# A recurrent attention followed by a top-1 mixture of experts: bonus coefficients from column-half matmuls of the transposed operands, and fp32 routing tables of two columns

## The chip, the cores and the metric

The kernel runs on one core of a Trainium2 chip. The metric is the device time of one execution in microseconds (us), from the first to the last instruction and what lies around them. Engines: PE (TensorE, matmuls; its weight loads are listed as PEld), DVE (VectorE), ACT (ScalarE), POOL (GpSimd) and SP (SyncE, which here only issues DMAs). Each engine works through its own list in order and waits on semaphores for the others.

## The reference

Two parts. An attention with a decaying state, over 4 batches, 8 heads, 768 positions and a head size of 48:

```python
for t in range(S):
    kt, vt, rt = (k[:, :, t], v[:, :, t], r[:, :, t])
    cur = np.einsum('bhd,bhe->bhde', u[None] * kt, vt)
    y[:, :, t] = np.einsum('bhd,bhde->bhe', rt, state + cur)
    state = w[None, :, :, None] * state + np.einsum('bhd,bhe->bhde', kt, vt)
```

The term with `u` is the bonus: position t's own v, times the number sum over d of r·u·k. This number is the bonus coefficient, one for each position and head. The result x (3072 rows of 384) goes through a top-1 mixture of 8 experts (384 to 1024 to 384, ReLU between): each row goes to the expert with the largest logit x @ w_gate, and its output is scaled by the softmax weight of that expert and by a sigmoid of x @ w_output_gate.

## The kernel before, in words

The rows are cut into 24 tiles of 128 positions (4 batches of 6). The main loop takes one step for each tile, about 6.5 us. While the attention of tile i is worked out, the operands of later tiles are prepared and the logits of tile i-1 are taken. The order of all work on each engine is written out by hand: the list STEP names the parts of a step, and the parts are emitted in that order, so that each engine gets its instructions in it.

What the parts do, with the lines of the profile:

- "sc" (L277): scores of tile i, K·R, from the transposed operands RT and KT, in 64-column halves, into the PSUM tiles ps_a (two buffers).
- "a0", "a1" (L281): DVE masks the two score tiles into A.
- "in" (L315): the part of the output from the state T, into ps_y. It waits until DVE has read ps_y of the tile before (L330).
- "xt" (L372, L374): three PE transposes of the output x of tile i-1 into a PSUM tile that shares the two buffers of ps_a, then the ACT copy xT.
- "tr" (L264, L265): PE transposes of the scaled K and R of tile i+1, and the ACT copies KT and RT.
- "lm" (L382, L386): logits of tile i-1 from xT (PE), and their ACT copy lg. At the end of a group of four to six tiles the routing program of the group is started.
- "i0", "i1" (L323): A·v into ps_y. "st" (L293 on PE, L301 or L298 on DVE, L302 on POOL): the new state. Its PSUM tile ps_u and the logits' tile ps_l share the one buffer with the tag "u".
- "p0", "p1" (L217): DVE scales R and K of tile i+2 by tables of powers of w.
- "ut" (L239, L240): POOL forms k·u·r for tile i+2, 128 positions by 384. "bo" (L249 on DVE, L251 on POOL): DVE reduces it to the coefficients of tile i+1, 128 by 8, and POOL multiplies v by them, which gives vc.
- at the end of the step DVE adds ps_y and vc to x (L330), and SP stores x (L335). "ld" issues the loads of tile i+3.
- "m": DVE's place for the routing program. Each "m" gives a credit of 0.25 or 0.3, and each piece of the routing costs 0.15 to 0.6 of it. "t1": the place for the routing's matmuls on PE.

The routing of a group ranks its rows in their experts and writes, for each place in an expert's list, the row's number and its weight into a table, by a matmul of two 0/1 matrices (L534, ps_tab). In bf16 a number needs several columns to stay exact: the row number takes two (tile and row) and the weight three (parts, L459 to L464), so the right side has 5 × 32 columns.

From tile 18 on, each step ends with two pieces of work on the first expert's weights: ACT rounds half a block (L758), POOL forms the rest (L759). In step 22 the routing of the fourth group ends, and POOL gathers the first 256 rows of the first expert (L781); step 23 transposes them (L793). After the loop come the last group's routing, with the first expert's matmuls among it, and then the experts one after another (from about 190 us to the end), which the change does not touch.

Of the kernel before, what the change touches and what calls it, by code (L numbers as in the profile page):

```python
# [41 lines left out]
HB = 64  # L42
ORDER_AT = 14
# [4 lines left out]
STEP = ['m', 'sc', 'a0', 'm', 'a1', 'in', 'xt', 't1', 'm', 'tr', 't1', 'ld', 'ut', 'bo', 'm', 'p0', 'm', 'p1', 'lm', 'i0', 'st', 'i1', 'm']  # L48
# [4 lines left out]
STEP0 = ['sc', 'a0', 'm', 'a1', 'in', 'tr', 'ld', 'bo', 'm', 'p0', 'm', 'p1', 'i0', 'st', 'i1', 'm']  # L53
# [94 lines left out]
def make_powers(tc, pool, k, halfway):  # L148
# [22 lines left out]
    k.pr, k.pk, k.w128 = pr, pk, sq[7]  # L171

# [10 lines left out]
def load_rkv(tc, pin, spare, srcs, b, c, first, after=None):  # L183
    nc = tc.nc
    ts = []
    for nm, s in zip("krv", (srcs[1], srcs[0], srcs[2])):
        if nm in first:
            t = first[nm][:, :, :D]
        elif spare:
            t = spare.pop(0).rearrange("p (h d) -> p h d", h=H)  # L190
        else:
            t = pin.tile([C, H, D], F32, name=f"{nm}_t")
        nc.sync.dma_start(t, s[b, :, c * C : (c + 1) * C, :].rearrange("h p d -> p h d"))
        ts.append(t)
        if after and nm == "k":
            after()
    return [ts[1], ts[0], ts[2]]


class Attention:  # L200
    def __init__(self, tc, ctx, k, load, x_d):
        self.tc, self.k = tc, k
        self.load, self.x_d = load, x_d
        self.pw = ctx.enter_context(tc.tile_pool(name="att_w", bufs=2))
        self.T = None
        self.st, self.ku, self.vc, self.A = {}, {}, {}, [None, None]
# [26 lines left out]
    def uterm(self, i):  # L233
        if i >= NT:
            return
        nc, k = self.tc.nc, self.k
        rt, kt, vt = self.load(i)
        ku = self.pw.tile([C, H, D], F32, name="ku")
        nc.gpsimd.tensor_mul(ku, kt, k.u_b.rearrange("p (h d) -> p h d", h=H))  # L239
        nc.gpsimd.tensor_mul(ku, ku, rt)  # L240
        self.ku[i] = ku

    def bonus(self, i):
# [3 lines left out]
        vt = self.load(i)[2]  # L247
        coef = self.pw.tile([C, H], F32, name="coef")
        nc.vector.tensor_reduce(out=coef, in_=self.ku.pop(i), axis=AX.X, op=ALU.add)  # L249
        vc = self.pw.tile([C, H, D], F32, name="vc")  # L250
        nc.gpsimd.tensor_mul(vc, vt, coef.unsqueeze(2).to_broadcast((C, H, D)))  # L251
# [87 lines left out]
class Router:  # L339
# [54 lines left out]
    def group(self, ps, w, lg, i0, G, closing, last):  # L394
# [41 lines left out]
        def weighting():  # L436
# [20 lines left out]
            rest = scale  # L457
            for i in range(3):
                nc.vector.tensor_copy(parts[:, i], rest)  # L459
                yield  # L460
                if i < 2:
                    nxt = mk(f"rest{i}")
                    nc.vector.tensor_sub(nxt, rest, parts[:, i])
# [9 lines left out]
        nc.tensor.matmul(cnt, k.tri, oh16.rearrange("p c e -> p (c e)"), start=True, stop=(G == 1 and (first or based)), skip_group_check=True)  # L473
        if not first and not based:
            nc.tensor.matmul(cnt, k.ones16, rep(self.csum16), start=False, stop=(G == 1), skip_group_check=True)
        for c in range(G - 1):
            nc.tensor.matmul(cnt[:, (c + 1) * E :], k.ones16, oh16[:, c, :].unsqueeze(1).to_broadcast((C, G - 1 - c, E)), start=False, stop=(c == G - 2), skip_group_check=True)
# [33 lines left out]
        sel = hold("sel", W, dt=BF16)  # L511
# [7 lines left out]
        ohp = hold("ohp", QP, dt=BF16)  # L519
# [3 lines left out]
        rhs = hold("rhs", 5, W, dt=BF16)  # L523
        (nc.vector if last else nc.gpsimd).tensor_mul(rhs[:, :, 0], sel, bc(k.tile0[:, cols], W))
        nc.scalar.activation(rhs[:, :, 1], sel, AF.Copy, scale=k.row1)
        tab = self.tab

        def columns(i):
            nc.vector.tensor_mul(rhs[:, :, 2 + i], sel, bc(parts[:, i], W))

        def product(lo, hi):
            pt = ps.tile([C, 512], F32, name="ps_tab", tag="g", bufs=1)
            for c in range(G):
                nc.tensor.matmul(pt[:, lo * W : hi * W], ohp[:, c, :], rhs[:, c, lo:hi].rearrange("p a w -> p (a w)"), start=(c == 0), stop=(c == G - 1), skip_group_check=True)  # L534
            return pt

        def collect(pt, i):
# [7 lines left out]
        if last:  # L545
            yield P
            pt = product(0, 2)
            for i in range(2):
                yield V
                collect(pt, i)  # L550
# [26 lines left out]
            pt = product(2, 5)
            for i in range(2, 5):
                yield V
                collect(pt, i)  # L580
# [21 lines left out]
        collect(pt, 4)
# [9 lines left out]
    def early(self, pb):  # L612
        nc, k = self.tc.nc, self.k
        nc.tensor.matmul(pb[:, :E], k.ones16, self.csum16, start=True, stop=True, skip_group_check=True)
        nc.vector.scalar_tensor_tensor(self.base, self.pm0, float(EARLY * QP), pb[:, :E], op0=ALU.mult, op1=ALU.max)

    def order(self, ps, w):
# [3 lines left out]
        nc.tensor.matmul(pt[:, :E], k.ones, self.csum, start=True, stop=True)  # L621
# [524 lines left out]
def rwkv_top1_moe(ctx, tc, r, kk, v, w, u, wg, wog, w1, w2, out):  # L1146
# [5 lines left out]
    load_w(tc, const, w, k)  # L1152
# [3 lines left out]
    with ExitStack() as actx:  # L1156
# [14 lines left out]
        u_b = const.tile([C, DM], F32, name="u_b")  # L1171
        k.u_b = u_b
        load(1, lambda: nc.sync.dma_start(u_b, u.rearrange("h d -> (h d)").unsqueeze(0).to_broadcast((C, DM))))
        rw = actx.enter_context(tc.tile_pool(name="rw", bufs=1))
        with tc.manual_schedule(engines=ORDERED):
# [5 lines left out]
                for nm, sh, dt in (("lg", (2 * E,), F32), ("oh", (E,), F32), ("ex", (E,), F32), ("oh16", (E,), BF16), ("sel", (NQ * E,), BF16), ("ohp", (QP,), BF16), ("rhs", (5, NQ * E), BF16))  # L1181
# [62 lines left out]
        with tc.If(fast == 1) as cmp:  # L1244
            with ExitStack() as fctx:
# [33 lines left out]
                att.uterm(0)  # L1279
                att.uterm(1)  # L1280
                x, X = None, {}

                for i in range(NT):
# [8 lines left out]
                    def act(a):  # L1292
# [14 lines left out]
                        elif a == "ut":  # L1307
                            att.uterm(i + 2)
# [95 lines left out]
```

## Time and profile before

| | us |
|---|---|
| median of 3 runs | 425.01 |
| lowest, highest | 418.87, 426.81 |
| the profiled execution | 422.51 |
| its span, first to last instruction | 420.8 |
| busy in the span: PE, DVE, ACT, POOL | 372.9, 256.6, 152.1, 165.5 |

A row of the profile's groups reads: line, engine, operation, tile written <- tiles read, shapes, count | busy time, mean of one in ns | idle time of the engine before them, and what ended it. A row of the timeline reads: start, duration, engine, line, operation, tiles, count [idle before <- what ended it]. Several instructions of one kind that follow each other are merged into one row. A matmul in fp32 shows as two records, so that eight matmuls are 16.

### The profile page before, as it was taken

What the parts mean: (1) busy time and instruction counts of PE and PEld (TensorE: products, weight loads), DVE (VectorE), ACT (ScalarE), POOL (GpSimd) and SP (SyncE); (2) the same over time, 40 slices, a digit from 0 to 9 for tenths busy, and PEclk for the clock granted to TensorE, in tenths of its full rate; (3) what the DMA queues carried; (4) which work ended last, traced back from release to release, by engine and by line L of the source; (5) the groups of instructions that cost most, each with busy time, mean ns of one, the idle gap of its engine ahead of it and who ended that gap; (6) DMA issues with size and microseconds to landing.
All of it is one profiled execution on the core that took longest, in us unless ns stands there. A gap on an engine that the chain in (4) does not pass through costs nothing. (4 is left out here: it accounts for less than half of the span.)

```text
span 420.8 us, 11171 instructions
## 1 busy us (share of the span) xinstructions
PE 372.9 (89%) x4500; PEld 352.2 (84%) x4500; DVE 256.6 (61%) x592; ACT 152.1 (36%) x310; POOL 165.5 (39%) x215
## 2 busy tenths in 40 slices
PE   7799789878967696995998999999999999999990
PEld 4688678777867695995997999999999999999980
DVE  5878898989988963552875266266363663636300
ACT  2223232223232332421455265264453553625210
POOL 6967456555556644524041032222313503301010
PEclk8899899989979866896999999999999999999996
DMA  8957566646686611045528165174273552830010
GB/s 135 174 130 162 106 149 142 141 104 134 142 213 176 153 58 58 20 134 168 151 66 280 38 210 169 43 239 157 65 241 129 185 191 88 261 122 34 2 43 18
DMA packets 104696, 55.01 MB, mean 131 GB/s; under 512 B 78511, under 2 KB 102243, under 8 KB 104624
## 3 DMA queue, kind: packets, MB, share of 16 engines
q1 hardware_dynamic: 101200, 44.27, 41.2%
q0 software_dynamic: 3424, 9.82, 6.9%
q8 instruction: 40, 0.66, 0.6%
q14 instruction: 32, 0.26, 0.2%
HBM read 44.64 MB, written 9.76 MB: 129 GB/s over the span
## 5 line engine op out<-in xcount | busy, mean ns | idle before, releaser
L847 POOL DMA_INDIRECT out_dram<-yo,si x28 | 28.7, 1026 | 134.1 <-ACT yo L844 72.7
L810 PE MATMUL ps_h<-xh,w1h 128*128 128x384 f32 (+4 forms) x216 | 74.7, 346 | 6.0 <-issue 4.7
L811 PE MATMUL ps_h<-xl,w1h 128*128 128x384 f32 (+4 forms) x216 | 72.5, 336 | 0.0
L812 PE MATMUL ps_h<-xh,w1l 128*128 128x384 f32 (+4 forms) x216 | 72.4, 335 | 0.0
L781 POOL DMA_INDIRECT xg<-x_d,gi x28 | 31.2, 1115 | 46.0 <-PE ps_xt L793 31.1
L810 PEld LDWEIGHTS ps_h<-xh,w1h 128*128 128x128 f32 x216 | 42.6, 197 | 7.4 <-issue 5.0
L820 DVE SCALAR_TENSOR_TENSOR hl<-ps_h,hh 128x384 fp32r<-128x384 f32 (+4 forms) x72 | 38.0, 533 | 17.2 <-ACT hh L819 16.8
L819 ACT ACTIVATE hh<-ps_h 128x384 fp32r<-128x384 f32 (+4 forms) x72 | 33.7, 472 | 32.7 <-PE ps_h L812 32.7
L374 ACT COPY xT<-ps_x 128x384 f32<-128x384 f32 x24 | 11.5, 479 | 91.7 <-PE ps_x L372 83.6
L872 PE MATMUL ps_o<-w2h,hh 128*128 128x384 f32 x128 | 43.5, 340 | 0.0
L873 PE MATMUL ps_o<-w2l,hh 128*128 128x384 f32 x128 | 42.9, 335 | 0.0
L811 PEld LDWEIGHTS ps_h<-xl,w1h 128*128 128x128 f32 x216 | 42.7, 198 | 0.1
L874 PE MATMUL ps_o<-w2h,hl 128*128 128x384 f32 x128 | 42.8, 334 | 0.0
L812 PEld LDWEIGHTS ps_h<-xh,w1l 128*128 128x128 f32 x216 | 42.6, 197 | 0.2
L759 DVE TENSOR_TENSOR w1l<-raw,w1h 128x768 fp32r<-128x768 f32 x28 | 26.7, 955 | 23.4 <-ACT w1h L758 21.0
L758 ACT CAST w1h<-raw 128x768 fp32r<-128x768 f32 (+1 forms) x36 | 27.1, 764 | 27.0 <-PE ps_h L811 19.9
L281 DVE TENSOR_TENSOR A<-ps_a,mask 128x512 f32<-128x512 f32 x48 | 31.3, 683 | 5.7 <-PE ps_a L277 5.7
L796 DVE TENSOR_TENSOR xl<-ps_xt,xh 128x384 fp32r<-128x384 f32 (+4 forms) x27 | 13.9, 538 | 32.4 <-ACT xh L795 32.1
L251 POOL TENSOR_TENSOR vc<-v_t,coef 128x384 f32<-128x384 f32 x21 | 21.3, 1014 | 28.0 <-DVE coef L249 18.1
L759 DVE TENSOR_TENSOR w2l<-raw,w2h 128x768 fp32r<-128x768 f32 x28 | 26.7, 958 | 7.4 <-ACT w2h L758 5.7
L758 ACT CAST w2h<-raw 128x768 fp32r<-128x768 f32 (+1 forms) x36 | 26.7, 765 | 8.4 <-PE ps_o L874 4.4
L323 PE MATMUL ps_y<-v_t,A 128*64 128x48 f32 x672 | 29.3, 237 | 0.0
(224 smaller groups left out, 784.4 us busy)
## 6 DMA issues: line engine op xcount, KB each, us to landing
raw<-in_moe_w_dram SPq DMA_DIRECT2D x64, 384.0 KB, 3.5
x_d<-x SPq DMA_DIRECT2D x24, 192.0 KB, 1.9
v_t<-in_v_dram SPq DMA_DIRECT2D x21, 192.0 KB, 4.7
k_t<-in_k_dram SPq DMA_DIRECT2D x20, 192.0 KB, 3.0
r_t<-in_r_dram SPq DMA_DIRECT2D x20, 192.0 KB
raw<-in_v_dram SPq DMA_DIRECT2D x3, 192.0 KB
raw<-in_k_dram SPq DMA_DIRECT2D x3, 192.0 KB
xg<-x_d,gi POOLq DMA_INDIRECT x28, 4.7
```

Of the source, the lines that this page charges most:

```text
L281: self.tc.nc.vector.tensor_mul(a, self.pa[j], self.k.mask.unsqueeze(1).to_broadcast((C, NP, C)))
L758: nc.scalar.copy(hi, self.raw[i][:, cs])
L759: (eng or nc.vector).tensor_sub(lo, self.raw[i][:, cs], hi)
L781: nc.gpsimd.indirect_dma_start(out=self.xg[q][:n], out_offset=None, in_=self.x_d[:n_x, :], in_offset=bass.IndirectOffsetOnAxis(ap=self.rt. ...
L810: nc.tensor.matmul(o, wh[:, j, fs], xh, start=(j == 0), stop=False)
L811: nc.tensor.matmul(o, wh[:, j, fs], xl, start=False, stop=False)
L812: nc.tensor.matmul(o, wl[:, j, fs], xh, start=False, stop=(j == KC - 1))
L819: nc.scalar.activation(hh, o, AF.Relu)
L820: nc.vector.scalar_tensor_tensor(hl, o, 0.0, hh, op0=ALU.max, op1=ALU.subtract)
L872: nc.tensor.matmul(o, hh, wh, start=(f == 0), stop=False)
L873: nc.tensor.matmul(o, hh, wl, start=False, stop=False)
L874: nc.tensor.matmul(o, hl, wh, start=False, stop=(f == FC - 1))
```

## The change

The bonus coefficients come from PE. A new part "pr" lets POOL form P = RT·KT of tile i+1, 128 by 512, in the transposed layout; RT and KT carry powers of w that leave a factor 1/w in their product, so the new constant uw holds u·w, one column for each of the two heads in a 128-row block. "bo" is now eight matmuls of 64 columns of P by two columns of uw, into a PSUM tile with the tag "u", then an ACT copy of the coefficients, and eight ACT instructions that scale v, one for each head. "ut", the DVE reduce and the POOL multiply are gone. The load of u as a 128-row broadcast becomes two small loads into ut, issued ahead of the loads of tile 1.

The step has another order: "tr" comes ahead of "xt", "lm" and both "t1" stand around "i0" and "st", "bo" comes last, and there are five "m" in place of six.

The routing tables are fp32 with two columns (row number, weight): the parts, two of the columns and their collecting adds are gone. The routing matmuls run as pairs of 64-column halves.

```diff
-STEP = ['m', 'sc', 'a0', 'm', 'a1', 'in', 'xt', 't1', 'm', 'tr', 't1', 'ld', 'ut', 'bo', 'm', 'p0', 'm', 'p1', 'lm', 'i0', 'st', 'i1', 'm']
+STEP = ['m', 'sc', 'a0', 'm', 'a1', 'in', 'tr', 'xt', 'pr', 'ld', 'm', 'p0', 'm', 'p1', 'lm', 't1', 'i0', 'st', 't1', 'i1', 'm', 'bo']
-STEP0 = ['sc', 'a0', 'm', 'a1', 'in', 'tr', 'ld', 'bo', 'm', 'p0', 'm', 'p1', 'i0', 'st', 'i1', 'm']
+STEP0 = ['sc', 'a0', 'a1', 'tr', 'in', 'pr', 'ld', 'p0', 'p1', 'i0', 'st', 'i1', 'bo']
...
+    k.uw = pool.tile([C, NP, 2], F32, name="uw")
+    nc.gpsimd.memset(k.uw, 0.0)
+    for j in range(2):
+        rows = slice(HB * j, HB * (j + 1))
+        nc.gpsimd.tensor_mul(k.uw[rows, :, j], k.ut[rows], sq[0][rows])
...
-    def uterm(self, i):
...
-        nc.gpsimd.tensor_mul(ku, kt, k.u_b.rearrange("p (h d) -> p h d", h=H))
-        nc.gpsimd.tensor_mul(ku, ku, rt)
+    def product(self, i):
...
+        self.P = self.pw.tile([C, NP, C], F32, name="P", bufs=1)
+        self.tc.nc.gpsimd.tensor_mul(self.P, RT, KT)
...
+        pb = ps.tile([C, 512], F32, name="ps_b", tag="u", bufs=1)
+        for q in range(NP):
+            for c in range(2):
+                half = slice(HB * c, HB * (c + 1))
+                nc.tensor.matmul(pb[half, 2 * q : 2 * q + 2], self.P[:, q, half], self.k.uw[:, q, :], start=True, stop=True)
         coef = self.pw.tile([C, H], F32, name="coef")
-        nc.vector.tensor_reduce(out=coef, in_=self.ku.pop(i), axis=AX.X, op=ALU.add)
+        nc.scalar.copy(coef, pb[:, :H])
+        vt = self.st[i][2]
         vc = self.pw.tile([C, H, D], F32, name="vc")
-        nc.gpsimd.tensor_mul(vc, vt, coef.unsqueeze(2).to_broadcast((C, H, D)))
+        for h in range(H):
+            nc.scalar.activation(vc[:, h, :], vt[:, h, :], AF.Copy, scale=coef[:, h : h + 1])
...
-            rest = scale
-            for i in range(3):
-                nc.vector.tensor_copy(parts[:, i], rest)
...
+        for hf in halves:
+            nc.tensor.matmul(cnt[hf], k.tri[:, hf], oh16.rearrange("p c e -> p (c e)"), start=True, stop=(G == 1 and (first or based)), skip_group_check=True)
...
-        rhs = hold("rhs", 5, W, dt=BF16)
+        rhs = hold("rhs", 2, W)
...
+                for hf in HALVES:
+                    nc.tensor.matmul(pt[hf, lo * W : hi * W], ohp[:, c, hf], rhs[:, c, lo:hi].rearrange("p a w -> p (a w)"), start=(c == 0), stop=(c == G - 1), skip_group_check=True)
...
-                            if i == 0:
-                                att.bonus(0)
-                                att.uterm(2)
-                            att.bonus(i + 1)
+                            att.bonus(ps, i + 1)
```

How this moves the instructions is shown at three places, before and then after. The first is PE in an early step without routing, from the state part of the output ("in", ps_y<-T,RT) to the next step's scores; ps_t are the transposes of "tr", ps_x those of "xt", ps_l the logits, ps_u the state. The line numbers are those of the two kernels. Before:

```order
L315 MATMUL ps_y<-T,RT 64x48 x16
L372 MATMUL ps_x<-ident,x 128x128 x3
L264 MATMUL ps_t<-ident,Kn_300 128x128 x4
L264 MATMUL ps_t<-ident,Rn_297 128x128 x4
L382 MATMUL ps_l<-wg_151,xT 64x16 x6
L323 MATMUL ps_y<-v_t,A_675 64x48 x8
L293 MATMUL ps_u<-v_t,Kn_299 64x48 x8
L323 MATMUL ps_y<-v_t,A_677 64x48 x8
L277 MATMUL ps_a_771<-RT,KT 64x128 x2
```

After, in the corresponding step:

```order
L323 MATMUL ps_y<-T,RT 64x48 x16
L272 MATMUL ps_t<-ident,Kn_307 128x128 x4
L272 MATMUL ps_t<-ident,Rn_304 128x128 x4
L380 MATMUL ps_x<-ident,x 128x128 x3
L390 MATMUL ps_l<-wg_153,xT 64x16 x6
L331 MATMUL ps_y<-v_t,A_867 64x48 x8
L301 MATMUL ps_u<-v_t,Kn_306 64x48 x8
L331 MATMUL ps_y<-v_t,A_869 64x48 x8
L253 MATMUL ps_b<-uw,P 64x2 x8
L285 MATMUL ps_a_978<-RT,KT 64x128 x2
```

The transposes of x now stand directly ahead of the logits that need their copy xT, where the eight transposes of "tr" stood between them before, and the eight bonus matmuls stand between the last A·v and the next scores.

The second place is ACT in a step without routing; KT, RT and xT are the copies of the transposes, lg that of the logits. In brackets are the semaphores that an instruction waits for, by engine. Before:

```order
L374 COPY xT<-ps_x 128x384 [waits PE_49,Activation_49]
L265 COPY KT<-ps_t 128x512 [waits PE_49]
L265 COPY RT<-ps_t 128x512 [waits PE_49]
L386 COPY lg_502<-ps_l 128x16 [waits PE_49]
L374 COPY xT<-ps_x 128x384 [waits PE_49,Activation_49]
```

After:

```order
L255 COPY coef<-ps_b 128x8 [waits PE_49]
L259 ACTIVATE vc<-v_t,coef 128x48 [waits DMAHW1_49,DVE_49,Activation_49]
L259 ACTIVATE vc<-v_t,coef 128x48 x7
L273 COPY KT<-ps_t 128x512 [waits PE_49,Pool_49]
L273 COPY RT<-ps_t 128x512 [waits PE_49]
L382 COPY xT<-ps_x 128x384 [waits PE_49]
L394 COPY lg_530<-ps_l 128x16 [waits PE_49]
```

The copy xT was first and is now behind KT and RT, and nine bonus instructions stand ahead of the three.

The third place is POOL from step 21 to the end of the loop; w1l and w2l are the pieces of the weights, xg the gathered rows, T the state. Before:

```order
L759 TENSOR_TENSOR w1l_79<-raw_71,w1h_78 128x384 x2
L251 TENSOR_TENSOR vc<-v_t,coef 128x384
L302 TENSOR_TENSOR T<-T_3174,sq_209 128x192
L781 DMA xg_110<-x_d,gi_173 128x384
L781 DMA xg_111<-x_d,gi_173 128x384
L759 TENSOR_TENSOR w2l_81<-raw_68,w2h_80 128x384 x2
```

After:

```order
L751 TENSOR_TENSOR w1l_79<-raw_71,w1h_78 128x384 x2
L773 DMA xg_110<-x_d,gi_175 128x384
L773 DMA xg_111<-x_d,gi_175 128x384
L243 TENSOR_TENSOR P<-RT,KT 128x512
L310 TENSOR_TENSOR T<-T_3516,sq_211 128x192
L751 TENSOR_TENSOR w2l_81<-raw_68,w2h_80 128x384 x2
```

The two gathers came behind the last state update of POOL and now stand ahead of the product P that the last bonus matmuls need.

More of the change, by code (lines that the diff above doesn't have):

```diff
@@ L472, in group @@
         based = last
[L473 to L477, printed above, removed]
+        halves = (slice(0, C),) if last else HALVES
+        for hf in halves:
+            nc.tensor.matmul(cnt[hf], k.tri[:, hf], oh16.rearrange("p c e -> p (c e)"), start=True, stop=(G == 1 and (first or based)), skip_group_check=True)
+            if not first and not based:
+                nc.tensor.matmul(cnt[hf], k.ones16[:, hf], rep(self.csum16), start=False, stop=(G == 1), skip_group_check=True)
+            for c in range(G - 1):
+                nc.tensor.matmul(cnt[hf, (c + 1) * E :], k.ones16[:, hf], oh16[:, c, :].unsqueeze(1).to_broadcast((C, G - 1 - c, E)), start=False, stop=(c == G - 2), skip_group_check=True)
         next(side, None)
@@ L522, in group, with weights @@
         yield Slot(0.3)
-        rhs = hold("rhs", 5, W, dt=BF16)
-        (nc.vector if last else nc.gpsimd).tensor_mul(rhs[:, :, 0], sel, bc(k.tile0[:, cols], W))
-        nc.scalar.activation(rhs[:, :, 1], sel, AF.Copy, scale=k.row1)
+        rhs = hold("rhs", 2, W)
+        (nc.vector if last else nc.gpsimd).tensor_mul(rhs[:, :, 0], sel, bc(k.id1[:, cols], W))
         tab = self.tab
-        def columns(i):
-            nc.vector.tensor_mul(rhs[:, :, 2 + i], sel, bc(parts[:, i], W))
+        def weights():
+            nc.vector.tensor_mul(rhs[:, :, 1], sel, bc(self.scale[:, cols], W))
         def product(lo, hi):
@@ L546, in group @@
             yield P
[L547 to L550, printed above, removed]
+            pt = product(0, 1)
+            yield V
+            collect(pt, 0)
             yield V
@@ L569, in group @@
             yield SPLIT
-            parts = w.tile([C, 3, G], BF16, name=f"parts_{G}", tag="parts")
             for _ in weighting():
                 yield V
-            for i in range(3):
-                columns(i)
-                yield V
+            weights()
             yield P
[L577 to L580, printed above, removed]
+            pt = product(1, 2)
+            yield V
+            collect(pt, 1)
             yield V
@@ L589, in group @@
             yield V
-        for i in range(3):
-            yield Slot(0.2)
-            columns(i)
+        yield Slot(0.2)
+        weights()
         yield P
-        pt = product(0, 5)
+        pt = product(0, 2)
         if closing:
-            self.early(pt[:, 5 * W :])
-        for a, b in ((0, 2), (1, 3)):
+            self.early(pt[:, 2 * W :])
+        for a in range(2):
             yield V
             collect(pt, a)
-            collect(pt, b)
-        yield V
-        collect(pt, 4)
         if closing:
@@ L620, in order @@
         pt = ps.tile([C, 512], F32, name="ps_ord", tag="g", bufs=1)
-        nc.tensor.matmul(pt[:, :E], k.ones, self.csum, start=True, stop=True)
+        for hf in HALVES:
+            nc.tensor.matmul(pt[hf, :E], k.ones[:, hf], self.csum, start=True, stop=True)
         yield V
@@ L1159, in rwkv_top1_moe, with load @@
         ready, pin = {}, []
-        def load(i, after=None):
+        def load(i):
             if i < NT and i not in ready:
-                ready[i] = load_rkv(tc, pin and pin[0], spare, (r, kk, v), *divmod(i, NCH), k.raw0 if i == 0 else {}, after)
+                ready[i] = load_rkv(tc, pin and pin[0], spare, (r, kk, v), *divmod(i, NCH), k.raw0 if i == 0 else {})
             return ready.get(i)
@@ L1278, in rwkv_top1_moe @@
                     att.prep(*a)
-                att.uterm(0)
-                att.uterm(1)
+                att.product(0)
+                att.bonus(ps, 0)
                 x, X = None, {}
```

59 lines of the change are left out of this document (23 added, 36 removed).

## The prediction

> **What bounds the kernel now.** I read the windows by stage first, to see where the change can matter. A row has the stretch, its length, the busy time of PE, PEld, DVE, ACT and POOL with counts, PE's granted clock, and the DMA share.
>
> ```profile
> 9.00:40.00 31.00, 27.75 (x694) 24.72 (x692) 24.83 (x41) 7.97 (x19) 24.36 (x30) 0.91 0.75 150
> 190.00:421.00 231.00, 214.02 (x1242) 209.78 (x1242) 107.99 (x190) 95.75 (x166) 54.69 (x51) 0.97 0.41 131
> ```
>
> From 190 us on PE is busy 214 of 231 us, and the change does not touch that. In the loop PE, DVE and POOL are all busy for about 25 of 31 us, and ACT for 8. Next, the ends of the steps, by DVE's rows of x (of tiles 1, 17 and 23):
>
> ```profile
> 22.82 0.56 DVE L330 TENSOR_TENSOR x<-ps_y,vc 128x384 f32<-128x384 f32 x1 [0.18 <-PE ps_y L323]
> 119.58 0.54 DVE L330 TENSOR_TENSOR x<-ps_y,vc 128x384 f32<-128x384 f32 x1
> 167.03 0.56 DVE L330 TENSOR_TENSOR x<-ps_y,vc 128x384 f32<-128x384 f32 x1 [1.12 <-PE ps_y L323]
> ```
>
> Steps 2 to 17 take 96.8 us, 6.05 each; steps 18 to 23 take 47.4, 7.9 each. Then PE's timeline of one step without routing:
>
> ```profile
> 32.99 1.10 PE L277 MATMUL ps_a<-RT,KT 48*64 48x128 f32 x32
> 33.91 0.63 PE L315 MATMUL ps_y<-T,RT 48*64 48x48 f32 x32
> 34.88 0.55 PE L372 MATMUL ps_x<-ident,x 128*128 128x128 f32 x3 [0.33 <-DVE A L281]
> 35.26 0.60 PE L264 MATMUL ps_t<-ident,Kn 128*128 128x128 f32 x4
> 35.70 0.60 PE L264 MATMUL ps_t<-ident,Rn 128*128 128x128 f32 x4
> 36.23 0.53 PE L382 MATMUL ps_l<-wg,xT 128*64 128x16 f32 x12
> 36.60 0.65 PE L323 MATMUL ps_y<-v_t,A 128*64 128x48 f32 x16
> 37.10 0.67 PE L293 MATMUL ps_u<-v_t,Kn 128*64 128x48 f32 x16
> 37.60 0.64 PE L323 MATMUL ps_y<-v_t,A 128*64 128x48 f32 x16
> 38.17 1.10 PE L277 MATMUL ps_a<-RT,KT 48*64 48x128 f32 x32
> ```
>
> From scores to scores it is 5.18 us, and the only wait is 0.33: a quiet step is bound by PE. Steps with routing are bound by DVE:
>
> ```profile
> 120.77 0.90 PE L372 MATMUL ps_x<-ident,x 128*128 128x128 f32 x3 [3.37 <-DVE A L281]
> 117.13:120.55 3.42, 0.27 (x12) 1.00 0.94 254
> 120.55:123.96 3.41, 3.19 (x23) 0.50 0.83 188
> ```
>
> PE waited 3.37 us for A, which stood behind routing on DVE, and in the next window PE's clock (the figure behind the count) was halved. On average a step up to 17 is 0.87 longer than a quiet one, 14 us over 16 steps: some 4.6 for each of the three groups in them.
>
> **What the change gives DVE and POOL.** The reduce leaves DVE, the three long products leave POOL:
>
> ```profile
> L281 DVE TENSOR_TENSOR A<-ps_a,mask 128x512 f32<-128x512 f32 x48 | 31.3, 683 | 5.7 <-PE ps_a L277 5.7
> L249 DVE TENSOR_REDUCE coef<-ku 128x8 f32<-128x384 f32 x24 | 13.0, 543 | 0.8 <-POOL ku L240 0.8
> 35.79 0.55 DVE L217 TENSOR_TENSOR Rn<-r_t,PR 128x384 f32<-128x384 f32 x1
> 36.26 1.18 DVE L217 TENSOR_TENSOR Kn<-k_t,PK 128x384 f32<-128x384 f32 x1
> 35.95 1.07 POOL L251 TENSOR_TENSOR vc<-v_t,coef 128x384 f32<-128x384 f32 x1 [0.26 <-DVE coef L249]
> L240 POOL TENSOR_TENSOR ku<-ku,r_t 128x384 f32<-128x384 f32 x20 | 20.1, 1007 | 1.7 <-DMA r_t<-in_r_dram 0.2
> L302 POOL TENSOR_TENSOR T<-T,sq 128x192 f32<-128x192 f32 x16 | 8.5, 531 | 21.6 <-DVE T L301 20.6 <-DVE gi L687 1.0
> ```
>
> DVE gains 0.54 us a step, and some 0.6 where its Kn (0.55 like Rn when alone) took 1.18 beside POOL's vc. POOL falls from 3 × 1.0 + 0.53 to P + 0.53; P of 512 elements, on the line through 384 (1.007) and 192 (0.531), is 1.32. A quiet step then has on DVE two masks of 0.68, Rn, Kn and x of 0.55 each and T of 0.36 (its row is below): 3.4 us. Routing loses five small operations, two of three weight columns and three of five collecting adds a group; its fp32 operands I cost like the bf16 ones, whose inputs are mostly fp32 already.
>
> **What it costs PE.** Eight bonus matmuls are 16 records; the 16 of A·v, also 64 columns of 128 rows, advance PE by 0.50 (36.60 to 37.10), the 12 of the logits by 0.37. I take 0.50 a step. They use the tag "u" and so wait until DVE has read ps_u:
>
> ```profile
> 37.89 0.36 DVE L301 TENSOR_TENSOR T<-ps_u,T 128x192 f32<-128x192 f32 x1 [0.45 <-PE ps_u L293]
> ```
>
> This read ends at 38.25, 0.08 after PE is free for the next scores: with a semaphore 0.13. The scores queue behind it.
>
> **The moved transposes.** This is the largest term. Now x's transposes come first and ACT copies xT while PE does "tr":
>
> ```profile
> 35.52 0.48 ACT L374 COPY xT<-ps_x 128x384 f32<-128x384 f32 x1 [3.65 <-PE ps_x L372]
> 35.90 0.58 ACT L265 COPY KT<-ps_t 128x512 f32<-128x512 f32 x1
> 36.38 0.59 ACT L265 COPY RT<-ps_t 128x512 f32<-128x512 f32 x1
> ```
>
> After the change, counted from the first transpose of K: KT starts at 0.64 (35.26 to 35.90, 0.04 after K's last transpose ends), RT 0.48 later, xT 0.48 after that, at 1.60, and ends at 2.08; with a semaphore the logits start at 2.13. PE itself is ready at 0.44 + 0.53 + 0.38 = 1.35 to 1.45. So PE waits 0.7 in each step for a copy that is hidden today, and both A·v, the state and the bonus matmuls queue behind the logits on PE. The wait for A (0.33) goes, since "tr" needs no buffer of A.
>
> Can ACT keep up? It has the copy of the coefficients and eight scaled copies of 48 elements ahead of KT. The nearest rows have a scale read from memory:
>
> ```profile
> L525 ACT ACTIVATE rhs<-sel,row 128x160 bf16<-128x160 bf16 x2 | 0.9, 435 | 0.0
> L525 ACT ACTIVATE rhs<-sel,row 128x128 bf16<-128x128 bf16 x2 | 0.8, 401 | 1.8 <-DVE rest L463 1.8
> 209.72 0.58 ACT L844 ACTIVATE yo<-ps_o,t 128x384 f32<-128x384 f32 x1 [3.55 <-PE ps_o L874]
> 210.19 0.99 ACT L795 CAST xh<-ps_xt 128x464 fp32r<-128x464 f32 x2
> ```
>
> With 34 ns for 32 elements, 48 take about 0.33; L844 shows that the next instruction starts 0.11 before the end. So I take 0.22 each; the bounds are 0.12 (the plain copies above, 0.48 and 0.38 for 512 and 384 elements, drawn down to 48) and 0.34 (no overlap), and L525 is nearest, since it too reads SBUF. From the start of the bonus matmuls: coefficients read at 0.7 to 0.9, eight copies issued by 2.7; KT can start at 0.50 + 0.92 + 0.64 + 0.64 = 2.70. So at 0.22 ACT is just in time; at 0.34 a step is 0.9 longer; at 0.12 nothing is won.
>
> A quiet step after: 0.50 bonus, 0.92 scores (32.99 to 33.91), 0.64 state (0.97 less the wait), 2.13 to the logits, then 0.37, 0.50, 0.50, 0.57 and the 0.13: 6.26, which I round to 6.3, against 5.18. P (RT copied by 3.8, then 1.32) is ready at 5.1, a microsecond before its use. x, due when the state part starts, has 1.42 us from the bonus matmuls on.
>
> **The clock.** The trace has these windows beside the two above:
>
> ```profile
> 42.04:45.45 3.41, 1.89 (x62) 1.00 0.65 141
> 45.45:48.87 3.42, 3.26 (x28) 0.50 0.91 183
> 52.28:55.69 3.41, 2.04 (x44) 1.00 0.51 121
> ```
>
> After 1.89 us busy of 3.41 the clock halved; after 2.04 it did not. The new step is idle 0.83 of 6.3, so no window falls under 2.5, and I cost the clock at nothing. The Trainium skill ("TensorE: Matmul & The Clock Gate", "A second HAM failure mode: psum-queue depth-cycling") says that frequent short idles between groups of matmuls can make the clock swing between half and full; by it this change would be much slower (rival 4). The trace's rows disagree: windows with less than full work kept the full clock.
>
> **The sum**, against the profiled execution (422.51, span 420.8):
>
> - Start: the first scores now wait for POOL's P, but the first state waited for DVE anyway; x of tile 1 within ±1 us: 0.
> - Steps 2 to 17: 16 × 6.3 = 100.8. Three groups' routing matmuls as half pairs in fp32: the product's five become 20 records at the 0.031 of A·v's, 0.62, and the counts double; I take 0.5 more each: 1.5. DVE late where P blocks it (the two scaled tiles behind a routing operation): 2. In all 104.3 against 96.8: +7.5. Routing itself then hardly lengthens a step: of 6.3 us DVE has 2.9 free, and a group's 4.6 spread over three steps.
> - Steps 18 to 23: the weights' two casts (the first row below) stand ahead of KT on ACT and cost up to 0.8 a step:
>
> ```profile
> 148.36 0.93 ACT L758 CAST w1h<-raw 128x384 fp32r<-128x384 f32 x2
> 158.78 1.23 POOL L781 DMA_INDIRECT xg<-x_d,gi  x1 [0.40 <-DVE sc L610]
> 160.31 1.00 POOL L781 DMA_INDIRECT xg<-x_d,gi  x1 [0.31 <-issue]
> 163.21 1.83 PE L793 MATMUL ps_xt<-ident,xg 128*128 128x128 f32 x6 [2.97 <-DMA xg<-x_d,gi]
> ```
>
> I take 6.8 for step 18 (6.3 and the third group's product), 7.2, 7.5, 7.7 and 7.2 for 19 to 22 (6.3 and 0.8; in 20 and 21 the fourth group's matmuls and DVE operations beside the pieces). The gathers (2.5 us, 158.78 to 161.3) are now ahead of P, and they start once POOL has done step 21's pieces, some 5.2 us into step 22; P ends at 9, so the last bonus matmuls wait 2 to 3 us, with the scores of step 23 behind them. But the rows land before PE needs them, so the 2.97 goes. Step 23 is that wait, then bonus, scores, state, six transposes of x and of the rows, A·v, and their copies on ACT and DVE ahead of x: 8.0 instead of the 8.65 of before (my estimate, the loosest of these). In all 44.4 against 47.4: -3.
> - Behind the wait of 2.97 the six transposes took 1.83 us, three times those of K: half clock. It would last less: -1.
> - SP: the loads of a tile keep their order; u's two small loads ahead of tile 1's take the place of one broadcast load: 0.
>
> Together +3.5: 426. The profiled run lies 2.5 under the median of 425.01, so the time is 428.5.
>
> **The rivals.**
>
> 1. Faster: the wait ahead of the logits is mostly hidden. Price: 16 × 0.5 off the first part, and with steps 18 to 23 at 6.5 each another 5: 428.5 - 13, with no late DVE -2, 413.5. It decides once that wait is under 0.25. For it: DVE's waits of 3.37 vanish, and PE's own work is only 5.45 a step. Against: ACT's order and its copies' durations are in the rows. 0.18.
> 2. ACT becomes the bound: the scaled copies take 0.34, 0.9 a step, 22 steps: 448. Against: the overlap of L844. 0.12.
> 3. DVE stays the bound in half of the steps: P and the weights' pieces block it as vc blocked Kn, T comes 1 us late in 12 steps, and the bonus matmuls with it: 440.5. 0.18.
> 4. The clock: short idles halve it in every second window. PE's 5.45 us of work in a step then take 5.45 / 0.75 = 7.3, 1.8 more, 40 over 22 steps: 468. 0.03. It is the case of the Trainium skill's page above.
>
> **How the numbers follow.** My forecast has 0.49, with 421 to 437 as its own range. The range over the cases, 412 to 443, leaves out 2, 4 and the edges. Two per cent, 8.5 us, is about what a measurement tells from no change. Faster by over that (under 416.5) is most of rival 1 and a little of mine: 0.18. Slower (over 433.5) is rivals 2, 3, 4 in the main and a tenth of mine: 0.34. Within: 0.48.
>
> **What would show it.** PE's logits would be released by ACT's xT in quiet steps, after some 0.7 us; quiet steps would be 6.3, and steps with routing hardly longer; the scaled copies would advance ACT by 0.22; PE's waits for A before x's transposes would be gone; at step 22 PE would wait for POOL's P. If quiet steps are 5.7 or the xT wait is missing, the main step is wrong.

## The result, and the profile after

| | before | after |
|---|---|---|
| median | 422.13 us (4 runs, 418.87 to 426.81) | 444.36 us (4 runs, 442.42 to 448.00) |
| profiled execution, its span | 422.51 us, 420.8 us | 442.42 us, 440.7 us |
| PE's granted clock, mean over the span | 0.935 | 0.918 |

The changed kernel is slower: the ratio is 1.056, its 95% interval 1.043 to 1.070. Ratios here and below compare undisturbed executions (within 1.5% of the fastest of the same kernel); medians are over all.

Again I began with the ends of the steps, DVE's rows of x for tiles 1, 17 and 23 in the timeline of the changed kernel:

```profile
23.55 0.56 DVE L338 TENSOR_TENSOR x<-ps_y,vc 128x384 f32<-128x384 f32 x1 [0.18 <-PE ps_y L331]
139.45 0.54 DVE L338 TENSOR_TENSOR x<-ps_y,vc 128x384 f32<-128x384 f32 x1
188.00 0.56 DVE L338 TENSOR_TENSOR x<-ps_y,vc 128x384 f32<-128x384 f32 x1 [1.06 <-PE ps_y L331]
```

The start is 0.7 us later than before, steps 2 to 17 took 115.9 us (before 96.8, forecast 104.3), steps 18 to 23 took 48.55 (before 47.4, forecast 44.4), and behind the loop 252.7 of the span are left, 1.1 less than before. So the forecast is missed by 11.6 in the long stretch and by 4.2 in the short one. The windows by stage show where (length, busy time of PE, PEld, DVE, ACT and POOL with counts, PE's clock, DMA):

```profile
9.00:40.00 31.00, 27.99 (x504) 25.39 (x502) 14.47 (x26) 15.20 (x51) 7.35 (x15) 0.69 0.57 118
20.66:24.07 3.41, 2.51 (x76) 2.41 (x76) 1.31 (x3) 0.94 (x3) 1.78 (x2) 1.00 0.66 131
24.07:58.20 34.13, 32.43 (x526) 30.80 (x524) 11.30 (x23) 13.69 (x48) 5.33 (x6) 0.50 0.41 90
75.27:78.69 3.42, 2.58 (x73) 2.29 (x65) 2.46 (x5) 3.23 (x11) 0.41 (x1) 1.00 0.90 199
```

DVE and POOL were relieved as planned: from 9 to 40 us DVE is busy for 14.5 us instead of 24.8, POOL for 7.4 instead of 24.4. But PE has 504 matmul records in that stretch where it had 694 before, at a clock of 0.69. From 24.07 to 58.20 us, ten windows of 3.41 us in a row, the clock stood at half, though PE was busy for 95% of the time. The window just ahead of it had 2.51 us of work in 3.41; the one at 75.27, in the middle of the loop, has 2.58 and is followed by full clock.

PE's timeline of the changed kernel, first a quiet step at full clock, then rows of one at half clock:

```profile
81.27 0.63 PE L253 MATMUL ps_b<-uw,P 128*64 128x2 f32 x16 [0.15 <-DVE tab L540]
81.83 1.10 PE L285 MATMUL ps_a<-RT,KT 48*64 48x128 f32 x32
82.75 0.63 PE L323 MATMUL ps_y<-T,RT 48*64 48x48 f32 x32
83.32 0.66 PE L272 MATMUL ps_t<-ident,Kn 128*128 128x128 f32 x4
83.81 0.60 PE L272 MATMUL ps_t<-ident,Rn 128*128 128x128 f32 x4
84.25 0.49 PE L380 MATMUL ps_x<-ident,x 128*128 128x128 f32 x3
85.57 0.53 PE L390 MATMUL ps_l<-wg,xT 128*64 128x16 f32 x12 [0.84 <-ACT xT L382]
85.94 0.65 PE L331 MATMUL ps_y<-v_t,A 128*64 128x48 f32 x16
86.42 0.64 PE L301 MATMUL ps_u<-v_t,Kn 128*64 128x48 f32 x16
86.89 0.64 PE L331 MATMUL ps_y<-v_t,A 128*64 128x48 f32 x16
87.68 0.40 PE L253 MATMUL ps_b<-uw,P 128*64 128x2 f32 x8 [0.16 <-DVE T L309]
```

```profile
33.24 1.00 PE L253 MATMUL ps_b<-uw,P 128*64 128x2 f32 x16
34.16 1.98 PE L285 MATMUL ps_a<-RT,KT 48*64 48x128 f32 x32
...
38.67 0.84 PE L380 MATMUL ps_x<-ident,x 128*128 128x128 f32 x3
40.08 0.83 PE L390 MATMUL ps_l<-wg,xT 128*64 128x16 f32 x12 [0.57 <-ACT xT L382]
...
43.32 0.47 PE L253 MATMUL ps_b<-uw,P 128*64 128x2 f32 x6
```

At full clock a step is 6.41 us (81.27 to 87.68), with the wait of 0.84 for xT; nothing waits for A any more. At half clock it is 10.08 (33.24 to 43.32), nearly three windows of 3.41. Steps 2 to 5 took 37.8 us in place of the forecast's 4 × 6.52 = 26.1 (104.3 us over 16 steps): these 11.7 us are the whole miss up to step 17.

The costs of the change itself, from the groups of instructions of the changed kernel, and its step 22 from the timelines of POOL and PE:

```profile
L259 ACT ACTIVATE vc<-v_t,coef 128x48 f32<-128x48 f32 x168 | 40.2, 321 | 0.8 <-DMA raw<-in_moe_w_dram 0.2
L243 POOL TENSOR_TENSOR P<-RT,KT 128x512 f32<-128x512 f32 x24 | 32.4, 1348 | 82.8 <-ACT RT L273 82.7
```

```profile
176.28 1.23 POOL L773 DMA_INDIRECT xg<-x_d,gi  x1 [0.17 <-issue]
177.82 1.00 POOL L773 DMA_INDIRECT xg<-x_d,gi  x1 [0.31 <-issue]
178.84 1.27 POOL L243 TENSOR_TENSOR P<-RT,KT 128x512 f32<-128x512 f32 x1
180.17 1.02 PE L253 MATMUL ps_b<-uw,P 128*64 128x2 f32 x16 [1.77 <-DVE x L338]
```

168 scaled copies keep ACT busy for 40.2 us, 0.24 each with their overlap; P takes 1.35 on average, 1.27 here. In step 22 the gathers hold P back, and the bonus matmuls wait 1.77 us; the row names x as what ended the wait, but P ended at 180.11, just ahead of their start. The kind of wait is as forecast, its length under the 2 to 3 us.

### The profile page after: what moved, and what is told of

Its sections match the earlier page's. It is cut to its first block, busy times and chain, and to the rows that moved or that the text cites. A ratio compares the mean times of both kernels' runs of the same rounds, so it can differ in the third digit from the quotient of the medians.

```text
span 440.7 us, 12294 instructions
## 1 busy us (share of the span) xinstructions
PE 394.0 (89%) x4998; PEld 375.2 (85%) x4998; DVE 225.5 (51%) x519; ACT 200.4 (45%) x521; POOL 125.4 (28%) x170
## 5 line engine op out<-in xcount | busy, mean ns | idle before, releaser
L802 PE MATMUL ps_h<-xh,w1h 128*128 128x384 f32 (+4 forms) x216 | 73.1, 338 | 4.1 <-issue 4.1
L803 PE MATMUL ps_h<-xl,w1h 128*128 128x384 f32 (+4 forms) x216 | 71.4, 331 | 0.0
L243 POOL TENSOR_TENSOR P<-RT,KT 128x512 f32<-128x512 f32 x24 | 32.4, 1348 | 82.8 <-ACT RT L273 82.7
L802 PEld LDWEIGHTS ps_h<-xh,w1h 128*128 128x128 f32 x216 | 41.5, 192 | 4.6 <-issue 4.4
L804 PEld LDWEIGHTS ps_h<-xh,w1l 128*128 128x128 f32 x216 | 41.4, 192 | 0.2
L803 PEld LDWEIGHTS ps_h<-xl,w1h 128*128 128x128 f32 x216 | 41.5, 192 | 0.1
L259 ACT ACTIVATE vc<-v_t,coef 128x48 f32<-128x48 f32 x168 | 40.2, 321 | 0.8 <-DMA raw<-in_moe_w_dram 0.2
L390 PEld LDWEIGHTS ps_l<-wg,xT 128*64 128x64 f32 x288 | 11.3, 149 | 26.5 <-ACT xT L382 26.5
L285 PE MATMUL ps_a<-RT,KT 48*64 48x128 f32 x768 | 32.3, 316 | 0.0
L390 PE MATMUL ps_l<-wg,xT 128*64 128x16 f32 x288 | 13.6, 220 | 20.4 <-ACT xT L382 20.4
```

The source lines that it names most:

```text
L243: self.tc.nc.gpsimd.tensor_mul(self.P, RT, KT)
L259: nc.scalar.activation(vc[:, h, :], vt[:, h, :], AF.Copy, scale=coef[:, h : h + 1])
L285: nc.tensor.matmul(self.pa[j][half, q, :], KT[rows, q, half], RT[rows, q, :], start=True, stop=True)
L802: nc.tensor.matmul(o, wh[:, j, fs], xh, start=(j == 0), stop=False)
L803: nc.tensor.matmul(o, wh[:, j, fs], xl, start=False, stop=False)
L804: nc.tensor.matmul(o, wl[:, j, fs], xh, start=False, stop=(j == KC - 1))
```

## The experiments

Each kernel ran beside the one before on the same chip.

| kernel | median, us | lowest to highest | ratio to before, 95% | clock of the profiled run |
|---|---|---|---|---|
| after, once more | 447.23 | 441.83 to 457.84 | 1.048 (1.039 to 1.057) | 0.879 |
| after, x's transposes first | 425.88 | 422.50 to 428.24 | 1.011 (1.006 to 1.016) | 0.950 |
| after, wait filled | 433.14 | 430.11 to 436.79 | 1.024 (1.005 to 1.042) | 0.966 |
| after, filled in steps 1 and 2 | 447.71 | 443.12 to 466.12 | 1.049 (1.041 to 1.056) | 0.918 |
| after, filled by one matmul | 437.55 | 432.30 to 448.10 | 1.024 (1.016 to 1.033) | 0.910 |
| after, vc on POOL | 443.24 | 429.73 to 458.90 | none | 0.953 |
| after, x first, vc on POOL, bonus inside | 419.53 | 416.54 to 422.59 | 0.991 (0.983 to 0.998) | 0.937 |
| before, x's transposes behind K's and R's | 429.32 | 427.71 to 431.85 | 1.016 (1.005 to 1.026) | 0.931 |
| before, routing part of after | 412.49 | 411.99 to 413.98 | 0.974 (0.970 to 0.979) | 0.964 |
| before, routing tables without halves | 419.44 | 416.43 to 421.98 | 0.984 (0.975 to 0.993) | 0.936 |

**x's transposes first.** One edit in the changed kernel:

```diff
-STEP = [..., 'in', 'tr', 'xt', 'pr', ...]
+STEP = [..., 'in', 'xt', 'tr', 'pr', ...]
```

> The changed kernel with one edit: x's transposes stand ahead of the K- and R-transposes again (xt before tr), as in the kernel before. Theory A (the order: x's transposes right ahead of the logits make PE wait 0.6 to 0.8 us for ACT's xT copy in each step, and this idle time is what tips the clock to half in steps 2 to 5): the wait of PE on xT ahead of the logits falls from 25.8 us to under 8 us, no run of half-clock windows longer than 10 us stands in steps 2 to 5, quiet steps at 5.5 to 5.9 us, time 415 to 427 us. Theory B (the half clock comes from the bonus matmuls, the routing halves or the start, not from the wait): the wait goes, but steps 2 to 5 still run at half clock, at 9 to 10 us each; time 428 to 440 us.

The time fell by 18 to 21 us (against the two medians of after). PE's timeline of one quiet step of this kernel, and the window that covers the ten half-clock windows of after:

```profile
38.50 0.63 PE L323 MATMUL ps_y<-T,RT 48*64 48x48 f32 x32
39.46 0.55 PE L380 MATMUL ps_x<-ident,x 128*128 128x128 f32 x3 [0.33 <-DVE A L289]
39.84 0.60 PE L272 MATMUL ps_t<-ident,Kn 128*128 128x128 f32 x4
40.28 0.60 PE L272 MATMUL ps_t<-ident,Rn 128*128 128x128 f32 x4
40.81 0.53 PE L390 MATMUL ps_l<-wg,xT 128*64 128x16 f32 x12
...
43.08 0.63 PE L253 MATMUL ps_b<-uw,P 128*64 128x2 f32 x16 [0.20 <-POOL P L243]
```

```profile
24.07:58.20 34.13, 30.01 (x824) 27.38 (x821) 20.52 (x55) 20.97 (x76) 8.98 (x10) 1.00 0.59 128
```

The wait for xT is gone, steps 2 to 17 ran wholly at full clock, and PE has 824 records where after has 526. So theory A holds for the time and the clock. A quiet step is 6.06 us, not 5.5 to 5.9: the wait for A is back (0.33), and the bonus matmuls now wait 0.2 for P, which starts only when RT has been copied, behind xT on ACT. At full clock the order is worth just 6.41 - 6.06 = 0.35 us a step, some 6 us over 16 steps; most of the rest is the half clock that went, with the mean clock up from 0.918 to 0.950.

**The wait kept, but filled.** The order of after, with matmuls on constants in the wait, whose sums nobody reads:

```diff
 X[i - 1] = rt.logits_t(ps, rw, x, "at", 2)
+att.fill(i)
...
+def fill(self, i):
+    if i % NCH > 0:
+        for _ in range(FILL):
+            self.tc.nc.tensor.matmul(self.y[:, 1, 256:], self.k.warm[:, :C], self.k.warm[:, :256], start=False, stop=False, skip_group_check=True)
```

> The changed kernel in its own order, with five bf16 matmuls of 256 columns, which depend on nothing that is late, between x's transposes and the logits (their sums go to columns of ps_y that nobody reads): the wait for xT stays in the chain, but PE is not idle in it. Theory A (idle PE time in that wait tips the clock): steps 2 to 5 run at full clock, quiet steps stay at 6.2 to 6.5 us, time 427 to 435 us, mean granted clock over 0.94. Theory B (the wait has nothing to do with the clock): steps 2 to 5 stay near 10 us, the clock at 0.92 or under, time 443 to 452 us.

The logits still wait for the same copy, and quiet steps stayed at 6.41 us. But steps 2 to 17 ran at full clock throughout, half clock fell to 20 us (from 12 to 210 us of the profiled execution; before 44, after 58), and the time fell by 11 to 14 us, although PE does more work. This separates the clock from the wait: with the wait left in the chain but PE busy in it, the long half-clock stretch goes, as theory A says.

Filling in steps 1 and 2 alone (`if i in (1, 2)`) asked whether it is one bad window that then holds:

> The changed kernel with the five filling matmuls of the second run, but only in steps 1 and 2. Theory L (the half clock is a latch: one dull window ahead of step 2 tips it, and the steps behind, though they run at the same waits at full clock later, are held there): steps 2 to 5 run at 6.2 to 6.7 us in nearly all executions, time 427 to 436 us. Theory M (the waits of each step tip it again wherever they are not filled): a run of half-clock steps stands in steps 3 to 8 all the same, time 438 to 450 us.

It is not: 447.7 us. In the profiled execution half clock came in steps 7, 13, 15 and 16 instead of 2 to 5, again 58 us of it. So it is no latch set ahead of step 2: waits that are not filled tip the clock in later steps too. Theory M has the time; the run that it put in steps 3 to 8 was two windows about step 7, and the unfilled steps 3 to 5 ran at full clock. An unfilled wait can tip the clock, but most do not.

One filling matmul instead of five (FILL = 1) asked how little is enough:

> The changed kernel with one filling matmul of 256 columns in each wait for xT instead of five. Over the ten profiles so far, of the windows of 3.41 us at full clock, none with PE busy for 2.6 us or more was followed by half clock, and of those between 1.5 and 2.6 some three in ten were. A quiet step of the changed kernel leaves windows of 2.46 to 2.64. Theory W (this edge decides): 0.1 to 0.15 us more of busy time in each wait lifts them to 2.65 to 2.8, quiet steps run at full clock at 6.3 to 6.5 us, half clock starts only in steps with routing or behind step 17; time 427 to 436 us. Theory V (the edge is a coincidence; it takes a wait that is filled altogether): long half-clock stretches in quiet steps as before, time 440 to 450 us.

Three windows of this kernel, one with the wait of a quiet step, one that came before half clock, and the one behind it:

```profile
83.00:86.41 3.41, 2.68 (x74) 2.35 (x67) 2.22 (x4) 3.06 (x11) 0.58 (x1) 1.00 0.53 129
35.19:38.61 3.42, 2.22 (x70) 2.13 (x71) 1.02 (x3) 1.16 (x4) 1.60 (x2) 1.00 0.63 123
38.61:42.02 3.41, 3.41 (x78) 3.30 (x76) 1.15 (x3) 2.08 (x9) 0.17 (x1) 0.50 0.20 65
```

A window with the one wait now has 2.68 us of work, and no such window was followed by half clock. It followed windows with more than that wait: a longer one (PE waited 1.05 us for xT in the one at 35.19), or a second of 0.15 to 0.83 ahead of the bonus matmuls. Three of five executions lie under 438 us, two at 447 and 448. The profiled one is the one at 448, and it has 61 us of half clock from 12 to 210 us, no less than after. So theory W holds for the windows with the one wait, and misses otherwise: its time was set too low, and half clock began in the quiet step 4 too (the window at 35.19), since other windows still fall under the edge.

**The order alone, in the kernel before.** There: `'in', 'tr', 'xt', 't1', 'm', 't1', 'ld'` in place of `'in', 'xt', 't1', 'm', 'tr', 't1', 'ld'`.

> The kernel before with the order alone: the K- and R-transposes ahead of x's (tr before xt), the bonus still on POOL and DVE, the routing tables as before. Theory A: quiet steps grow from 5.2 by the 0.6 to 0.7 us of the xT wait, and a run of half-clock windows of over 15 us stands in the loop; time 432 to 447 us. Theory B (the bonus matmuls or the tables tip the clock): quiet steps grow by 0.3 to 0.7 us at the most, no run of half-clock windows over 10.3 us; time 420 to 431 us.

The row of the logits in a quiet step of this kernel:

```profile
42.40 0.53 PE L382 MATMUL ps_l<-wg,xT 128*64 128x16 f32 x12 [0.78 <-ACT xT L374]
```

Quiet steps went from 5.18 to 5.57 us: 0.78 for xT, less the 0.33 for A. No half-clock stretch exceeded 10.3 us. By its bounds theory B, and theory A failed: the order alone does not bring the long stretch. Here the wait leaves 3.41 - 0.78 = 2.63 us of busy time in a window that contains it, in the changed kernel 3.41 - 0.84 = 2.57. That is too small a difference to lean on. What this kernel lacks beside it are the bonus matmuls, which theory B names, and the count below shows that they matter: the long stretch came with the wait and these matmuls together, not with the wait alone (this kernel), nor with the matmuls alone (x's transposes first).

**vc on POOL.** The eight scaled copies of after back to `nc.gpsimd.tensor_mul(vc, vt, coef...)`.

> The changed kernel with vc made by one multiply on POOL (about 1.0 us, as before) in place of eight scaled copies on ACT (1.91 us). Theory A: the clock in steps 2 to 5 does not change, since PE still waits for xT behind its own transposes; steps 18 to 23, where the scaled copies and the 0.91 us of casts stand ahead of the KT copy, lose 0.5 to 1.2 us each; time 434 to 442 us. Theory C (ACT's scaled copies make xT late, and this is the wait that tips the clock): quiet steps fall to 5.8 to 6.1 us, steps 2 to 5 run at full clock, time 418 to 430 us.

Two executions took 430 and 432 us, two 454 and 459; no ratio comes from that. The wait for xT was 0.84 in the profiled one as well, so ACT's scaled copies don't make it, and theory C falls. Theory A missed too: in that execution steps 2 to 5 ran at full clock with the same wait of 0.84, and no execution lies in its 434 to 442. The kernel shows what the clock costs by itself: same program, clocks of 0.953, 0.938, 0.884 and 0.863, 29.2 us between the ends, 3.2 us for each 0.01.

**After once more.**

> The changed kernel itself once more. If the half clock of steps 2 to 5 belongs to its order, every execution shows a mean granted clock under 0.935 and a time of 438 to 450 us. If it is a matter of chance which execution falls into it, as with vc on POOL (two executions at 430 and 432 us with clocks of 0.953 and 0.938, two at 454 and 459 with 0.884 and 0.863), some lie under 434 us with a clock over 0.94.

All four lie at 441.8 us or above, with clocks from 0.879 to 0.929: the half clock belongs to this kernel, while its extent varies from execution to execution. Again 16.0 us for 0.050 of clock, 3.2 for each 0.01.

**The routing part alone, in the kernel before.** fp32 tables of two columns and the halves; bonus and order of before.

> The kernel before with the routing part alone: fp32 tables of two columns and the routing matmuls in two halves of columns; order and bonus as before. Theory A (this part is small, the loss comes from the order and what it does to the clock): time within 1% of before, 419 to 428 us, half-clock stretches as before, none over 10.3 us. Theory E (the routing halves hold PE, and a good part of the loss is theirs): routing steps longer by 0.5 us or more each, time 430 to 440 us.

Neither: it is faster than both kernels, by 12 us against before. The x of tiles 1, 17 and 23 in its timeline, and the windows over steps 2 to 17 and 18 to 23:

```profile
21.21 0.56 DVE L331 TENSOR_TENSOR x<-ps_y,vc 128x384 f32<-128x384 f32 x1 [0.18 <-PE ps_y L324]
115.21 0.55 DVE L331 TENSOR_TENSOR x<-ps_y,vc 128x384 f32<-128x384 f32 x1
158.22 0.55 DVE L331 TENSOR_TENSOR x<-ps_y,vc 128x384 f32<-128x384 f32 x1
```

```profile
21.77:115.76 93.99, 81.64 (x2140) 73.11 (x2129) 82.24 (x193) 26.48 (x70) 56.55 (x64) 0.98 0.66 144
115.76:158.77 43.01, 35.60 (x772) 31.59 (x772) 30.27 (x78) 14.09 (x36) 27.15 (x30) 0.84 0.54 140
```

Against before, steps 2 to 17 are 2.8 us shorter, 18 to 23 4.4 us, the start 1.6 us. Half clock fell from 44 to 20 us. Not all of the gain is the clock: steps 9 to 17, without half clock here and with one such window before, took 51.7 us against 55.5, DVE's busy time in them 46.3 against 50.4.

To see what the halves do, the same kernel without them (`HALVES = (slice(0, C),)`):

> The kernel before with the fp32 tables of two columns alone, without the halves: the routing matmuls over all 128 columns at once. Theory A (the gain of the routing part is DVE's and POOL's saved operations and the windows at half clock that these avert; the halves neither cost nor gain): 409 to 417 us, as with the halves (412.5). Theory H (the halves carry the gain, since two matmuls run side by side in the array): 418 to 427 us. Theory P (the halves cost PE 0.5 us a group and product, as forecast): 403 to 409 us.

419.4 us, between the theories' bands. In steps at full clock the two are equal (steps 9 to 17 of the profiles, with routing in them and no half clock: 51.7 us with the halves, 51.6 without), so the halves don't lengthen the steps as I forecast, nor shorten them there. What differs is half clock again, 20 us against 44, and the clocks of the four executions each do not overlap (0.955 to 0.967 with the halves, 0.927 to 0.944 without). Whether the halves cause that, or chance does, I did not settle; the intervals of the two ratios overlap.

**The bonus inside the step.** x's transposes first, vc on POOL, and the bonus matmuls of a tile behind the scores of its own step:

```diff
-STEP = ['m', 'sc', 'a0', ..., 'in', 'tr', 'xt', 'pr', ..., 'i1', 'm', 'bo']
+STEP = ['m', 'sc', 'bi', 'a0', ..., 'in', 'xt', 'tr', 'pr', ..., 'i1', 'm']
...
+elif a == "bi":
+    att.bonus(ps, i)
```

> The changed kernel with three edits: x's transposes ahead of the K- and R-transposes, vc by one multiply on POOL, and the bonus matmuls of a tile not at the end of the step before but behind the scores of its own step, where P has long been there and PE waits 0.3 to 0.5 us for DVE's A anyway. Theory A (what the change costs at full clock is waits, of PE for xT and for P, not the work of the bonus matmuls): quiet steps fall from 6.06 us (x's transposes first alone) to 5.2 to 5.6 us, the waits of PE for P (14.3 us in 18 times) go, time 405 to 418 us. Theory D (the bonus matmuls' 0.55 us and the rest of PE's work hold the step): quiet steps stay over 5.8 us, time 420 to 427 us.

Quiet steps are 5.56 us and PE never idles in them: 5.56 is PE's own work. The kernel before needs 5.18 with a wait of 0.33, so with these matmuls on PE a quiet step is 0.38 longer even without a wait. Theory A holds for the quiet step (5.2 to 5.6); the time lies between the two theories' bands, with 44 us of half clock, most of it behind step 17. 419.5 does not reach the 412.5 of the routing part alone.

By medians, from two sessions, the parts stack like this: before 424.7, the routing part -12 (412.5), the bonus on PE +13 (425.9, x's transposes first), x's transposes behind K's and R's +21 (447.2, after once more). The +13 is not split: it holds the bonus matmuls, the scaled copies on ACT and the new places of "lm", "t1" and "m". The same exchange of the transposes cost the kernel before only 4.5 us (429.3 against 424.8), so the parts do not simply add.

## Why the prediction was wrong

444.4 is 16 us over the forecast and just beyond the range's end of 443; the chance of slower was 0.34.

**The step that failed** is the one on the clock: "The new step is idle 0.83 of 6.3, so no window falls under 2.5, and I cost the clock at nothing." Both facts were nearly right: the step idles for 0.84 + 0.15, and quiet windows hold 2.57 and more (2.51 just ahead of the half clock). The conclusion was wrong. I had put the edge between 1.89 (halved) and 2.04 (not), from one window each, and I took the bonus matmuls for work like any other. Counted over the twelve profiles of this study, in the whole windows of 3.413 us laid on the clock's own changes from 12 to 210 us:

| PE busy in a window at full clock | windows | followed by half clock |
|---|---|---|
| under 1.5 us | 25 | 25 |
| 1.5 to 2.0 us | 21 | 11 |
| 2.0 to 2.6 us, no bonus matmul in it | 62 | 3 |
| 2.0 to 2.6 us, bonus matmuls in it | 28 | 20 |
| over 2.6 us | 387 | 0 |

The highest that was followed by half clock had 2.59, the lowest that was not 1.53. Without bonus matmuls the edge that I had read was not far off: none of the 42 such windows from 2.31 to 2.6 was followed by half clock. Of the windows with bonus matmuls, 10 of 18 there were. The changed kernel's own profile shows it at equal busy time. Seven windows with PE busy for 2.57 to 2.58 us and no bonus matmul, the one at 75.27 among them, kept full clock; the two ahead of half clock with nearly the same busy time, at 20.66 (2.51) and 136.71 (2.57), both hold the wait for xT and all the bonus matmuls of a step. PE's busy time on the bonus matmuls alone in two of these windows:

```profile
20.66:24.07 3.41, 0.55 (x16) 1.00 0.66 131
75.27:78.69 3.42, 0.00 (x0) 1.00 0.90 199
```

A third window with all of them (105.99, busy for 2.59) kept full clock, so the count gives odds, not a rule. A window of the kernel before with the wait for A alone:

```profile
62.51:65.93 3.42, 3.09 (x115) 2.91 (x114) 2.92 (x9) 0.17 (x1) 1.99 (x4) 1.00 0.39 93
```

It has 3.09. Filled by 0.1 us, a window with the wait for xT alone has over 2.6 and stays at full clock. That the idle time of the wait is needed for the long half-clock stretch is shown by the kernel with the wait filled by five matmuls and by x's transposes first, and that it is not enough by itself by the kernel before with x's transposes moved. That the bonus matmuls, of two columns each, hold the clock up less than other work is a count; no run changed these matmuls alone, and why they should stays open.

The Trainium skill ("TensorE: Matmul & The Clock Gate", "A second HAM failure mode: psum-queue depth-cycling") says that frequent short idles between groups of matmuls make the clock swing. I noted that the trace disagreed; the trace had too few such windows to say so, and in the changed kernel the clock did swing. My rival 4, at 0.03, was the nearest to the mechanism: half clock in 34 of the 116 us of steps 2 to 17, not in every second window, which is why the time is 444 and not 468.

Point by point:

- Quiet step 6.3: 6.41 at full clock. The wait for xT 0.7: 0.84. Bonus matmuls 0.50: 0.56. Their wait for ps_u 0.13: 0.15. The wait for A is gone. Steps 6 to 17, nearly all at full clock, took 78.1 us; 12 steps at the forecast's 6.52 (104.3 over 16) are 78.2.
- Scaled copies 0.22: 0.24; P 1.32: 1.35. Rival 2 (ACT the bound) did not come, nor rival 3: DVE idled 25 us ahead of A.
- Steps 18 to 23: 48.55 against 44.4. The last bonus matmuls waited 1.77 (forecast 2 to 3), and the gathers' wait of 2.97 went. Step 21 is at full clock in PE's timeline of the changed kernel:

```profile
163.84 1.10 PE L285 MATMUL ps_a<-RT,KT 48*64 48x128 f32 x32
...
168.27 0.53 PE L390 MATMUL ps_l<-wg,xT 128*64 128x16 f32 x12 [1.52 <-ACT xT L382]
...
171.46 1.10 PE L285 MATMUL ps_a<-RT,KT 48*64 48x128 f32 x32
```

  From scores to scores it is 7.62, against 7.7: the casts make the wait for xT 1.52 instead of 0.84, 0.68 more, against "up to 0.8". The 4.2 too many came with 20.5 us of half clock in steps 18 to 20, 22 and 23, some 7.4 us by the 3.2 for each 0.01 of clock (an estimate). The windows ahead of it hold waits for xT of 0.84, 1.64 and 1.52 us: the same failed step. But the kernel before had 23.1 us of half clock in these steps, so there the clock explains the miss of the forecast, which counted these steps as if at full clock, and not the loss against before.
- Behind the loop -1: -1.1. Start 0: +0.7.
- The routing part: I gave its matmuls +1.5 and let the savings on DVE vanish in the longer quiet step. Alone it is worth -12, which the sum never showed as a term of its own.

Against before, not the forecast, the clock is the smaller part: 0.935 against 0.918, at 3.2 us for 0.01, is 5.4 of the 20 us between the profiled executions. The rest is longer steps: a quiet one grew by 1.23 us, 0.35 by the order and 0.88 by the bonus on PE (0.56 of matmuls, 0.2 of wait for P, the rest small gaps, by the kernel with x's transposes first).

## What to carry to other kernels

When PE is the bound, price an idle stretch twice: its own length, and what it leaves of work in a clock window, with the edge counted over many windows rather than read from one. Ask too what the busy time of the window is made of: at 2.51 to 2.59 us the changed kernel kept the clock in all seven windows without bonus matmuls, and lost it in two of three with all of a step's. Time a change's parts apart before the whole: here a gain of 12 us was hidden under two losses, and that part alone beats both kernels.

## What was unexpected of the hardware

At half clock, busy time alone does not bring full clock back. Of 161 half-clock windows in the twelve profiles, none of the 31 with PE busy for under 3.05 us was followed by full clock; of the other 130, most of them busy from end to end, 66 were. Here too the bonus matmuls set windows apart: of these 130, 48 held some of them, and 10 were followed by full clock; of the 82 without, 56 were. In the ten windows from 24.07 us on, every third holds the xT wait, 0.57 us at that clock, and the step of 10.08 us keeps pace with three windows (10.24); seven of the ten hold bonus matmuls or that wait. What sets apart the rest stayed open. The Trainium skill ("TensorE: Matmul & The Clock Gate", "What's actually happening") names one idle window for the fall and one busy window for the rise; here windows of 45 to 76% busy time brought the fall in 34 of 111 cases, and busy ones the rise in half.
